# Router logits of an attention and mixture-of-experts kernel: four float32 matmuls against twelve bfloat16 ones on three exact parts

## The chip, the cores and the metric

One core of a Trainium2 chip runs the whole program in one launch. The metric is the device time of an execution in microseconds (us). The engines named below are TensorE (PE, with its weight loads PEld), VectorE (DVE), ScalarE (ACT), GpSimd (POOL) and SyncE (SP), which issues most transfers.

## What is computed

Three layers follow each other: banded attention with a few "sink" keys, a mixture of experts with one expert for each token, and a feed-forward layer with a leaky ReLU. The change lies in the router of the second:

```python
def _moe_ref(x, expert_emb, tau, w1, w2):          # x 1536x512, expert_emb 8x512
    xn = x / (np.linalg.norm(x, axis=-1, keepdims=True) + 1e-06)
    en = expert_emb / (np.linalg.norm(expert_emb, axis=-1, keepdims=True) + 1e-06)
    logits = xn @ en.T / tau
    expert_idx = np.argmax(logits, axis=1)
    ...
    gate_w = probs[np.arange(N), expert_idx]
    for e in range(E):
        mask = expert_idx == e
        h = np.maximum(x[mask] @ w1[e], 0.0)
        out[mask] = gate_w[mask, None] * (h @ w2[e])
```

Tokens go to the expert with the largest logit, so the logits need close to float32 precision.

## The kernel before

**Attention** (function `attention`) takes 2 batches x 2 head groups x 6 query blocks x 4 heads, 96 steps of a software pipeline. A step issues one score (L261, two float32 matmuls), on VectorE the masked scores with their minimum (L266), on ScalarE the exponential a step later (L268), five steps later the transposes of the probabilities (L280, copied by L283) and ten steps later the product with the values (L298, L301) of a block. VectorE then divides by the sums (`finish`: L310, L311, L312), which gives the tile `x` of 128 tokens; with the second head group x has its 512 columns. Between these steps the heads of the next group are transposed (L196) and split (L202, L207, L216, L217).

**The router** handles twelve tiles of 128 tokens, in two batches of six that come with the second head group of each batch of attention. `router_turn` (L690) transposes x in four pieces (L697) into one PSUM tile and copies it to SBUF (ScalarE, L700); `router_logits` (L709) multiplies the four pieces with the turned embeddings `embT` (L716, 128x8), takes the maximum in the pass that reads the logits out of PSUM (L718), and makes the index and one-hot row of the expert (L720 to L724). The last tile, number 11, is turned in two halves. PSUM tiles: four of tag "t" (all transposes), three of tag "sc" (scores, logits, ranks), one for xp.

**After the last tile** `router_rank` and `rank_experts` (L727, L751) count tokens for each expert and write the experts' numbers in the order of work, `eid` (L772). SyncE reads these numbers into registers and issues the loads of the experts' weights (`fetch`, L997) with them; the experts' matmuls (L1079) and the feed-forward layer follow, with the weights split into two parts by ScalarE and VectorE (L1001, L1002).

The order of each engine's instructions in the attention part is not written by hand: the program is scheduled at build time, by dependences and estimated times, so an added operation can move others.

Of the kernel before, what the change touches and what calls it, by code (L numbers as in the profile page):

```python
# [7 lines left out]
F32 = mybir.dt.float32  # L8
F32R = mybir.dt.float32r
BF16 = mybir.dt.bfloat16  # L10
# [5 lines left out]
ALU = mybir.AluOpType  # L16
AX = mybir.AxisListType
# [4 lines left out]
P = 128  # L22
# [3 lines left out]
E = 8  # L26
# [112 lines left out]
def attention(c, ctx):  # L139
# [152 lines left out]
    def value(b, g, i):  # L292
# [25 lines left out]
        if g == 0 and half:  # L318
            later(3, lambda: router_turn(c, t, None, (0, 1)))
        if g == 1:  # L320
            later(3, lambda: router_turn(c, t, None, (2, 3) if half else (0, 1, 2, 3)))
            later(5, lambda: router_logits(c, t))
            if t in RANKS:
                t0 = RANKS[RANKS.index(t) - 1] + 1 if RANKS.index(t) else 0
                if t == NTT - 1:
                    later(7, lambda: rank_experts(c))
                later(7, lambda: router_rank(c, t0, t + 1))
# [13 lines left out]
    load_v(0, 0, 3, 3)  # L341
    first, second = group_turns(0, 0)
    setting = router_setup(c, ctx)
    stir(7)
    n = len(items)
# [248 lines left out]
def router_setup(c, ctx):  # L594


    nc, tc = c.nc, c.tc
    cp = c.const
    rp, emb, tau = c.embs
# [10 lines left out]
    t = c.pst.tile([P, 4, E], F32, tag="t", name="embT_ps")  # L610
    for kk in range(4):
        nc.tensor.transpose(t[:, kk, :], emb[:, kk * P:(kk + 1) * P], c.ident[0:E, 0:E])
    c.embT = cp.tile([P, 4, E], F32, name="embT")
    nc.vector.tensor_copy(c.embT, t)

    yield
    c.tri = cp.tile([P, P], BF16, name="tri")
# [69 lines left out]
    return y  # L687


def router_turn(c, t, pool=None, parts=(0, 1, 2, 3)):  # L690

    nc = c.nc
    pool = pool or c.pst
    x = c.x[t].rearrange("p h d -> p (h d)")
    tp = pool.tile([P, len(parts), P], F32, tag="t", name=f"xTp{c.uid()}")
    for k, kk in enumerate(parts):
        turned = nc.tensor.transpose(tp[:, k, :], x[:, kk * P:(kk + 1) * P], c.ident)  # L697
    if parts[0] == 0:
        c.xT[t] = c.rt.tile([P, 4, P], F32, tag="xT" if parts[-1] == 3 else "xTh", name=f"xT{c.uid()}", bufs=2 if parts[-1] == 3 else 1)
    first = nc.scalar.copy(out=c.xT[t][:, parts[0]:parts[-1] + 1], in_=tp)  # L700
    if parts[-1] == 3:
        c.x.pop(t)
        c.xT[t] = c.xT[t], turned
        sq = c.rt.tile([P, DM], F32, tag="sq", name=f"sq{c.uid()}", bufs=1)
        with c.tc.issue_after(first.ins):
            nc.scalar.activation(out=sq, in_=x, func=AF.Square, accum_out=c.ss[:, t:t + 1])


def router_logits(c, t, pool=None):  # L709

    nc = c.nc
    xT, turned = c.xT.pop(t)
    lp = (pool or c.psc).tile([P, E], F32, tag="sc", name=f"lg{c.uid()}")
    with c.tc.issue_after(turned.ins):
        for kk in range(4):
            nc.tensor.matmul(lp, lhsT=xT[:, kk, :], rhs=c.embT[:, kk, :], start=(kk == 0), stop=(kk == 3))  # L716
    lg, top, idx, oh = c.lg[:, t, :], c.top[:, t], c.idx[:, t:t + 1], c.oh[:, t, :]
    nc.vector.tensor_scalar(out=lg, in0=lp, scalar1=0.0, scalar2=None, op0=ALU.add, op1=ALU.max, accum_out=top)  # L718
    hit = c.rt.tile([P, E], F32, tag="hit", name=f"hit{c.uid()}")
    nc.vector.scalar_tensor_tensor(out=hit, in0=lg, scalar=top, in1=c.em8, op0=ALU.is_equal, op1=ALU.mult)  # L720
    nc.vector.tensor_reduce(out=idx, in_=hit, axis=AX.X, op=ALU.min)
    nc.vector.tensor_scalar(out=oh, in0=c.em8, scalar1=idx, scalar2=None, op0=ALU.is_equal)
    if t + 1 < NTT:
        nc.vector.tensor_tensor(out=c.cum[:, t + 1, :], in0=c.cum[:, t, :], in1=oh, op=ALU.add)  # L724
# [807 lines left out]
```

## Time and profile before

| | |
|---|---|
| median of 3 runs | 617.88 us (617.36 to 618.19) |
| the profiled execution | 617.09 us |
| its span, first to last instruction | 615.3 us |
| TensorE busy | 590.1 us (96%) |
| VectorE busy | 390.6 us (63%) |
| ScalarE busy | 288.8 us (47%) |
| mean granted TensorE clock | 0.97 of full speed |

Of the page, the busy shares say which engine is full over the whole span, and the chain of waits which engine's work ended last, step by step back from the end. A share over the span mixes stages; the table of stretches gives the busy time of each engine within one. The timeline gives single instructions with start and duration; neighbours on an engine can overlap a little.

### The profile page before, as it was taken

The numbers are of one execution on the slowest core, as the hardware profiler recorded it, in microseconds if no ns is written. First come the engines' busy times: TensorE is split into PE (matmuls) and PEld (weight loads), VectorE is DVE, ScalarE is ACT, GpSimd is POOL, SyncE is SP. The second block draws the span as 40 slices with busy tenths as digits, with TensorE's granted clock in tenths as the row PEclk, the third lists the DMA queues.
The fourth block names the chain that finished last, engine by engine and source line by source line (L and its number), as shares of the span: only waits on it lengthen the run. The fifth ranks groups of instructions, "written<-read, shape, count | busy, mean of one in ns | idle before, by whom it ended". The sixth has DMA issues, their size and how long they took to land.

```text
span 615.3 us, 9556 instructions
## 1 busy us (share of the span) xinstructions
PE 590.1 (96%) x3411; PEld 512.6 (83%) x3412; DVE 390.6 (63%) x915; ACT 288.8 (47%) x522; POOL 54.2 (9%) x156
## 2 busy tenths in 40 slices
PE   7899999997699999999999999999999999999996
PEld 4799999895499998889989888888888888888884
DVE  7889788856699659997974699964322223322240
ACT  4777787755688444624753445333312222322130
POOL 3011013003122010001000000000100001100001
PEclk7899999996699999999999999999999999999998
DMA  5777570013999593369599600000100000100001
GB/s 121 180 164 169 136 170 2 2 57 115 339 359 312 187 315 116 123 222 364 174 322 347 273 0 2 0 1 0 69 1 1 0 1 17 52 1 1 0 13 60
DMA packets 87991, 73.66 MB, mean 120 GB/s; under 512 B 54024, under 2 KB 70408, under 8 KB 87936
## 3 DMA queue, kind: packets, MB, share of 16 engines
q1 hardware_dynamic: 85824, 66.22, 34.7%
q0 software_dynamic: 2112, 6.75, 3.1%
q8 instruction: 29, 0.48, 0.3%
q14 instruction: 26, 0.21, 0.1%
HBM read 66.67 MB, written 6.29 MB: 119 GB/s over the span
## 4 chain that ended last, share of the span: by engine, by line
PE 88%; DMA 5%; DVE 3%; issue 1%; ACT 1%; POOL 0%; SPq 0%; POOLq 0%; DVEq 0%
PE hp L1079 32%; PE acc L1079 31%; PE xp L298 6%; PE sc L261 4%; DMA slot_raw<-in_moe_w 3%; PE tp L280 3%; PE acc L1188 2%; PE hp L1176 2%; PE lg L716 1%; PE tq L196 1%; PE xp L301 1%; PE xTp L697 1%; PE tr L1068 1%; PE tk L196 1%; DVE p L266 1%
## 5 line engine op out<-in xcount | busy, mean ns | idle before, releaser
L1079 PE MATMUL acc<-slot,h 128*128 128x512 f32 x588 | 146.2, 396 | 1.3 <-issue 1.3
L1079 PE MATMUL hp<-fxT,slot 128*128 128x512 f32 x576 | 140.9, 396 | 0.0
L1079 PEld LDWEIGHTS acc<-slot,h 128*128 128x128 f32 x588 | 109.8, 188 | 27.4 <-issue 1.5
L1079 PEld LDWEIGHTS hp<-fxT,slot 128*128 128x128 f32 x576 | 108.1, 188 | 26.2
L1426 DVE TENSOR_TENSOR lk<-hp,lk 128x512 f32<-128x512 f32 x48 | 32.9, 690 | 103.4 <-ACT lk L1425 103.3
L1425 ACT ACTIVATE lk<-hp 128x512 f32<-128x512 f32 x48 | 28.5, 598 | 119.9 <-PE hp L1079 111.3
L1002 DVE TENSOR_TENSOR slot<-slot_raw,slot 128x1024 fp32r<-128x1024 f32 x48 | 58.4, 1222 | 12.2 <-ACT slot L1001 11.5
L1001 ACT CAST slot<-slot_raw 128x1024 fp32r<-128x1024 f32 x48 | 50.1, 1049 | 19.7 <-DMA slot_raw<-in_moe_w 19.4
L268 ACT ACTIVATE p<-p,los 128x288 f32<-128x288 f32 (+2 forms) x96 | 45.7, 506 | 16.8 <-DVE los L266 16.1
L1079 PE MATMUL acc<-h,slot 128*128 128x256 f32 (+2 forms) x288 | 49.0, 319 | 0.0
L261 PE MATMUL sc<-head_k,head_q 128*128 128x288 f32 (+1 forms) x192 | 43.8, 338 | 4.0 <-DVE head_k L207 2.2
L1079 PEld LDWEIGHTS acc<-h,slot 128*128 128x128 f32 x288 | 43.1, 188 | 2.9
L298 PE MATMUL xp<-v,pt 128*128 128x65 f32 x352 | 43.8, 269 | 0.0
L298 PEld LDWEIGHTS xp<-v,pt 128*128 128x128 f32 x352 | 42.6, 192 | 0.1
L1428 DVE TENSOR_TENSOR h<-lk,h 128x512 fp32r<-128x512 f32 x43 | 29.5, 690 | 18.0 <-ACT h L1427 17.9
L1460 POOL DMA_INDIRECT out_y<-y,sid x12 | 11.7, 978 | 317.5 <-DVE y L1459 295.9
L1427 ACT CAST h<-lk 128x512 fp32r<-128x512 f32 x43 | 26.7, 622 | 27.1 <-DVE lk L1426 27.1
L261 PEld LDWEIGHTS sc<-head_k,head_q 128*128 128x128 f32 x192 | 29.8, 201 | 7.3 <-ACT head_q L216 3.4
L1079 PE MATMUL hp<-slot_big,slot 128*128 128x256 f32 (+1 forms) x192 | 35.4, 334 | 0.0
L1079 PEld LDWEIGHTS hp<-slot_big,slot 128*128 128x128 f32 x192 | 29.8, 189 | 2.7
L280 PE MATMUL tp<-ident,p 128*128 128x128 f32 x176 | 30.2, 278 | 0.0
L1095 POOL DMA_INDIRECT rows<-xd,ids x16 | 18.3, 1142 | 114.4 <-PE tr L1068 109.1
(252 smaller groups left out, 850.5 us busy)
## 6 DMA issues: line engine op xcount, KB each, us to landing
slot_raw<-in_moe_w SPq DMA_DIRECT2D x56, 512.0 KB
slot_wide<-in_moe_w_in SPq DMA_DIRECT2D x8, 1024.0 KB
slot_wide<-in_moe_w_out SPq DMA_DIRECT2D x8, 1024.0 KB
raw_q<-in_q SPq DMA_DIRECT2D x64, 96.0 KB
slot_first<-in_moe_w SPq DMA_DIRECT2D x8, 512.0 KB
raw_k<-in_k SPq DMA_DIRECT2D x32, 96.0 KB
xd<-x SPq DMA_DIRECT2D x12, 256.0 KB
v<-in_v SPq DMA_DIRECT2D x12, 192.0 KB
```

Of the source, the lines that this page charges most:

```text
L261: nc.tensor.matmul(sc[:, 0:w], lhsT=qt[:, half, i * P:(i + 1) * P], rhs=kt[:, off:off + w], start=half == 0, stop=half == 1)
L268: later(1, lambda: nc.scalar.activation(out=p, in_=p, func=AF.Exp, scale=-1.0, bias=lo))
L280: nc.tensor.transpose(u.t[:, h % 2, n, :], u.p[:, h, o:o + P], c.ident)
L298: nc.tensor.matmul(xp[:, h, :], lhsT=u.pt[h // 2][:, h % 2, n, :], rhs=vT[b, g][:, kb, h, :], start=h == 0 and n == 0, stop=h == 3 and i < ...
L1001: nc.scalar.copy(out=sl.g[0], in_=sl.raw)
L1002: nc.vector.tensor_tensor(out=sl.g[1], in0=sl.raw, in1=sl.g[0].bitcast(F32), op=ALU.subtract)
L1079: c.nc.tensor.matmul(out, lhsT=a[x], rhs=b[y], start=first and n == 0, stop=last and n == 2)
L1095: c.nc.gpsimd.indirect_dma_start(out=t[0:w], out_offset=None, in_=c.xd[:, :], in_offset=bass.IndirectOffsetOnAxis(ap=c.ids[0:w, q0 + k:q0 ...
L1425: nc.scalar.activation(out=raw, in_=hp, func=AF.Copy, scale=0.01)
L1426: nc.vector.tensor_tensor(out=raw, in0=hp, in1=raw, op=ALU.max)
L1427: x = nc.scalar.copy(out=h[:, 0, :], in_=raw)
L1428: y = nc.vector.tensor_tensor(out=h[:, 1, :], in0=raw, in1=h[:, 0, :].bitcast(F32), op=ALU.subtract)
```

## The change

The embeddings are split once into three bfloat16 parts that sum to the float32 value. Each tile of x is split the same way while it leaves PSUM: ScalarE casts it to bfloat16, VectorE subtracts that from the original (`left`, float32); the upper 16 bits of each number of `left` are the second part, read in place with a step of two; VectorE subtracts them, which gives the third. Three groups of four bfloat16 matmuls, one for each part of x, multiply with all three parts of the embeddings at once (24 columns). VectorE sums the three results of each expert and takes the maximum in a pass of its own. The first part and the last share a tile of tag "xT" with two buffers, `left` has two of its own; tile 11's separate buffer of tag "xTh" is gone.

```diff
@@ router_setup
     c.embT = cp.tile([P, 4, E], F32, name="embT")
     nc.vector.tensor_copy(c.embT, t)
+    c.emb3 = cp.tile([P, 4, 3, E], BF16, name="emb3")
+    left = rp.tile([P, 4, E], F32, name="emb_left")
+    nc.scalar.copy(out=c.emb3[:, :, 0], in_=t)
+    nc.vector.tensor_tensor(out=left, in0=c.embT, in1=c.emb3[:, :, 0], op=ALU.subtract)
+    nc.scalar.copy(out=c.emb3[:, :, 1], in_=left)
+    nc.vector.tensor_tensor(out=c.emb3[:, :, 2], in0=left, in1=c.emb3[:, :, 1], op=ALU.subtract)
@@
+def upper(t):
+
+    return t.bitcast(BF16).rearrange("p k (n t) -> p k n t", t=2)[:, :, :, 1]
@@ router_turn
     if parts[0] == 0:
-        c.xT[t] = c.rt.tile([P, 4, P], F32, tag="xT" if parts[-1] == 3 else "xTh", name=f"xT{c.uid()}", bufs=2 if parts[-1] == 3 else 1)
-    first = nc.scalar.copy(out=c.xT[t][:, parts[0]:parts[-1] + 1], in_=tp)
+        c.xT[t] = (c.rt.tile([P, 2, 4, P], BF16, tag="xT", name=f"xT{c.uid()}", bufs=2),
+                   c.rt.tile([P, 4, P], F32, tag="xl", name=f"xl{c.uid()}", bufs=2))
+    two, left = c.xT[t]
+    some = slice(parts[0], parts[-1] + 1)
+    mid = upper(left)[:, some]
+    first = nc.scalar.copy(out=two[:, 0, some], in_=tp)
+    nc.vector.tensor_tensor(out=left[:, some], in0=tp, in1=two[:, 0, some], op=ALU.subtract)
+    nc.vector.tensor_tensor(out=two[:, 1, some], in0=left[:, some], in1=mid, op=ALU.subtract)
@@ router_logits
-    lp = (pool or c.psc).tile([P, E], F32, tag="sc", name=f"lg{c.uid()}")
+    lp = (pool or c.psc).tile([P, 3, E], F32, tag="sc", name=f"lg{c.uid()}")
+    parts = [two[:, 0], upper(left), two[:, 1]]
     with c.tc.issue_after(turned.ins):
-        for kk in range(4):
-            nc.tensor.matmul(lp, lhsT=xT[:, kk, :], rhs=c.embT[:, kk, :], start=(kk == 0), stop=(kk == 3))
+        for n, x in enumerate(parts):
+            for kk in range(4):
+                nc.tensor.matmul(lp.rearrange("p a e -> p (a e)"), lhsT=x[:, kk, :], rhs=c.emb3[:, kk].rearrange("p a e -> p (a e)"),
+                                 start=n + kk == 0, stop=n + kk == 5)
-    nc.vector.tensor_scalar(out=lg, in0=lp, scalar1=0.0, scalar2=None, op0=ALU.add, op1=ALU.max, accum_out=top)
+    nc.vector.tensor_reduce(out=lg, in_=lp.rearrange("p a e -> p e a"), axis=AX.X, op=ALU.add)
+    nc.vector.tensor_reduce(out=top, in_=lg, axis=AX.X, op=ALU.max)
```

In the rows of the new order below, L717 and L718 are the two subtractions of `router_turn` (`xl` is `left`), L739 and L740 the sum and the maximum of `router_logits`, and all lines of the program after L612 stand some lines lower than before (the one-hot steps L720 to L724 are L742 to L746, the rank steps L736 to L743 are L758 to L765).

VectorE where the first batch's last two tiles meet the scores of attention, before: L721 to L724 finish the tile before, L266 are masked scores, L207 and L217 head splits.

```order
L721 TENSOR_REDUCE idx<-hit_1533 128x1
L207 TENSOR_TENSOR head_k_142<-tk_1552,head_k_142 64x384
L266 ISA p_1503,los<-sc_1558,mb 128x288
L266 ISA los 128x1
L207 TENSOR_TENSOR head_k_144<-tk_1552,head_k_144 64x384
L722 TENSOR_SCALAR oh<-em_685,idx 128x8
L724 TENSOR_TENSOR cum<-cum,oh 128x8
L266 ISA p_1582,los<-sc_1583,mc 128x288
L266 ISA los 128x1
L266 ISA p_1582,los<-sc_1626,mc 128x288
```

The same place now:

```order
L717 TENSOR_TENSOR xl_1553<-xTp_1547,xT_1552 128x512
L312 TENSOR_TENSOR x_1001<-xp_1578,rec_1583 128x256
L266 ISA p_1560,los<-sc_1609,mb 128x288
...
L744 TENSOR_SCALAR oh<-em_691,idx 128x8
L217 SCALAR_TENSOR_TENSOR head_q_143<-tq_1690,head_q_143 128x384
L718 TENSOR_TENSOR xT_1552<-xl_1553 128x512
L746 TENSOR_TENSOR cum<-cum,oh 128x8
L717 TENSOR_TENSOR xl_1638<-xTp_1632,xT_1637 128x512
L310 TENSOR_SCALAR rec_1712<-xp_1702 128x4
L718 TENSOR_TENSOR xT_1637<-xl_1638 128x512
L266 ISA p_1651,los<-sc_1652,mc 128x288
```

Four subtractions over 128x512, two tiles' worth, now stand between the last scores of one query block (mask `mb`) and the first of the next (`mc`).

VectorE at the last two tiles now; x_2081 is tile 11, xl_2475 tile 10, xl_2108 the second half of tile 11:

```order
L717 TENSOR_TENSOR xl_2475<-xTp_2469,xT_2474 128x512
L310 TENSOR_SCALAR rec_2486<-xp_2481 128x4
L758 TENSOR_TENSOR sel_2458<-rk_2455,oh 128x32
L718 TENSOR_TENSOR xT_2474<-xl_2475 128x512
L311 RECIPROCAL rec_2486<-rec_2486 128x4
L759 TENSOR_REDUCE r<-sel_2458 128x4
L312 TENSOR_TENSOR x_2081<-xp_2481,rec_2486 128x256
L762 TENSOR_TENSOR ge_2461<-t_695,r 128x44
L739 TENSOR_REDUCE lg<-lg_2487 128x8
...
L717 TENSOR_TENSOR xl_2108<-xTp_2511,xT_2107 128x256
L744 TENSOR_SCALAR oh<-em_691,idx 128x8
L718 TENSOR_TENSOR xT_2107<-xl_2108 128x256
```

Before, the L310 to L312 of tile 11 had only the rank steps between them; now both subtractions of tile 10 stand ahead of tile 11's L312.

## Rows read from the trace of the kernel before

**Rows 1.** The page, parts 1 and 4: busy time by engine; the chain by engine.
```profile
PE 590.1 (96%) x3411; PEld 512.6 (83%) x3412; DVE 390.6 (63%) x915; ACT 288.8 (47%) x522; POOL 54.2 (9%) x156
PE 88%; DMA 5%; DVE 3%; issue 1%; ACT 1%; POOL 0%; SPq 0%; POOLq 0%; DVEq 0%
```

**Rows 2.** Stretches: from:to length, busy PE, PEld, DVE, ACT, POOL, clock, DMA, GB/s.
```profile
60.00:97.00 37.00, 37.00 (x324) 36.37 (x323) 31.02 (x132) 30.03 (x72) 4.13 (x21) 1.00 0.52 130
61.70:84.10 22.40, 22.40 (x197) 21.97 (x195) 16.97 (x72) 17.55 (x44) 1.99 (x11) 1.00 0.54 144
84.10:96.00 11.90, 11.90 (x110) 11.90 (x108) 11.38 (x51) 10.93 (x27) 1.76 (x8) 1.00 0.53 122
97.00:120.00 23.00, 22.44 (x179) 20.90 (x178) 20.38 (x83) 16.74 (x40) 5.90 (x11) 1.00 0.01 2
120.00:137.00 17.00, 17.00 (x149) 16.68 (x148) 8.87 (x45) 10.12 (x28) 0.59 (x2) 1.00 0.13 47
137.00:146.00 9.00, 8.26 (x69) 7.87 (x68) 5.69 (x34) 3.41 (x9) 1.78 (x3) 0.91 0.23 88
```

**Rows 3.** Timeline (start, duration), and the last row from the chain.
```profile
148.46 0.15 DVE L772 CAST eid<-ef 1x8 int32<-1x8 f32 x1
149.63 25.95 SPq L997 DMA_DIRECT2D slot_raw<-in_moe_w  x19
...
153.98 9.55 DMA slot_raw<-in_moe_w
```

**Rows 4.** Timeline, TensorE: one tile's logits and the instruction after.
```profile
87.13 0.96 PE L716 MATMUL lg<-embT,xT 128*128 128x8 f32 x8
87.94 0.42 PE L697 MATMUL xTp<-ident,x 128*128 128x128 f32 x2
```

**Rows 5.** 16-bit weight loads: timeline of L791, and line L896 (min/median/max ns).
```profile
150.90 0.42 PEld L791 LDWEIGHTS <-slot_u 128*128 128x128 f16 x11 [0.27 <-issue]
151.24 0.13 PEld L1273 LDWEIGHTS <-hot 128*128 128x128 bf16 x2
...
L896 PEld LDWEIGHTS <-hot x12: 95/98/98, 284.0 to 284.4; 128*128 128x128 bf16 x12
```

**Rows 6.** Groups of instructions, VectorE, 0 to 170 us: busy us, mean ns, idle before.
```profile
L718 DVE TENSOR_SCALAR_CACHE_REDUCE lg<-lg 128x8 f32<-128x8 f32 x12 | 2.0, 165 | 1.6 <-PE cnt L759 0.8 <-PE lg L716 0.6
L721 DVE TENSOR_REDUCE idx<-hit 128x1 f32<-128x8 f32 x12 | 1.9, 159 | 0.1
L1073 DVE TENSOR_TENSOR mxT<-tr,mxT 128x512 fp32r<-128x512 f32 x1 | 0.7, 692 | 2.2 <-ACT mxT L1072 2.2
L1231 DVE TENSOR_TENSOR h<-th,h 128x256 fp32r<-128x256 f32 x1 | 0.4, 419 | 0.0
L834 DVE TENSOR_REDUCE mn<-ee 128x8 f32<-128x64 f32 x1 | 0.2, 220 | 0.0
```

**Rows 7.** Timeline, VectorE: a copy over 128x512 and what follows it.
```profile
87.56 0.69 DVE L283 COPY pt<-tp 128x512 f32<-128x512 f32 x1
88.15 0.16 DVE L718 TENSOR_SCALAR_CACHE_REDUCE lg<-lg 128x8 f32<-128x8 f32 x1
```

**Rows 8.** Timeline, the last tiles: tile 9's cast, tile 10's x, tile 11.
```profile
138.25 0.59 ACT L700 COPY xT<-xTp 128x512 f32<-128x512 f32 x1 [2.16 <-PE xTp L697]
...
140.88 0.42 DVE L312 TENSOR_TENSOR x<-xp,rec 128x256 f32<-128x256 f32 x1
...
143.09 0.42 DVE L312 TENSOR_TENSOR x<-xp,rec 128x256 f32<-128x256 f32 x1
...
143.57 0.44 PE L697 MATMUL xTp<-ident,x 128*128 128x128 f32 x2
...
144.04 0.37 ACT L700 COPY xT<-xTp 128x256 f32<-128x256 f32 x1 [1.00 <-PE xTp L697]
...
145.53 0.17 DVE L718 TENSOR_SCALAR_CACHE_REDUCE lg<-lg 128x8 f32<-128x8 f32 x1 [0.82 <-PE cnt L759]
```

**Rows 9.** Timeline, VectorE: the first batch's first rank step.
```profile
97.52 0.21 DVE L736 TENSOR_TENSOR sel<-rk,oh 128x48 f32<-128x48 f32 x1
```

More of the change, by code (lines that the diff above doesn't have):

```diff
@@ L698, in router_turn @@
     if parts[0] == 0:
-        c.xT[t] = c.rt.tile([P, 4, P], F32, tag="xT" if parts[-1] == 3 else "xTh", name=f"xT{c.uid()}", bufs=2 if parts[-1] == 3 else 1)
-    first = nc.scalar.copy(out=c.xT[t][:, parts[0]:parts[-1] + 1], in_=tp)
+        c.xT[t] = (c.rt.tile([P, 2, 4, P], BF16, tag="xT", name=f"xT{c.uid()}", bufs=2),
[6 more added lines that the diff above has]
+    nc.vector.tensor_tensor(out=two[:, 1, some], in0=left[:, some], in1=mid, op=ALU.subtract)
     if parts[-1] == 3:
         c.x.pop(t)
-        c.xT[t] = c.xT[t], turned
+        c.xT[t] = two, left, turned
         sq = c.rt.tile([P, DM], F32, tag="sq", name=f"sq{c.uid()}", bufs=1)
@@ L711, in router_logits @@
     nc = c.nc
-    xT, turned = c.xT.pop(t)
-    lp = (pool or c.psc).tile([P, E], F32, tag="sc", name=f"lg{c.uid()}")
+    two, left, turned = c.xT.pop(t)
+    lp = (pool or c.psc).tile([P, 3, E], F32, tag="sc", name=f"lg{c.uid()}")
+    parts = [two[:, 0], upper(left), two[:, 1]]
     with c.tc.issue_after(turned.ins):
-        for kk in range(4):
-            nc.tensor.matmul(lp, lhsT=xT[:, kk, :], rhs=c.embT[:, kk, :], start=(kk == 0), stop=(kk == 3))
+        for n, x in enumerate(parts):
+            for kk in range(4):
+                nc.tensor.matmul(lp.rearrange("p a e -> p (a e)"), lhsT=x[:, kk, :], rhs=c.emb3[:, kk].rearrange("p a e -> p (a e)"),
+                                 start=n + kk == 0, stop=n + kk == 5)
     lg, top, idx, oh = c.lg[:, t, :], c.top[:, t], c.idx[:, t:t + 1], c.oh[:, t, :]
-    nc.vector.tensor_scalar(out=lg, in0=lp, scalar1=0.0, scalar2=None, op0=ALU.add, op1=ALU.max, accum_out=top)
+    nc.vector.tensor_reduce(out=lg, in_=lp.rearrange("p a e -> p e a"), axis=AX.X, op=ALU.add)
+    nc.vector.tensor_reduce(out=top, in_=lg, axis=AX.X, op=ALU.max)
     hit = c.rt.tile([P, E], F32, tag="hit", name=f"hit{c.uid()}")
```

## The prediction

> **What bounds the kernel now.** I read the page first: engine shares and the chain of waits [rows 1]. TensorE is busy 96% of the span and holds 88% of the chain, so work taken off it can count, but only where it is the last to arrive. Then the stretches [rows 2]. The router's twelve tiles come in two batches of six: the first within 60 to 97 us, the second from 123 to 146 us. In both the reader is to compare TensorE with VectorE. From 60 to 97 us TensorE is busy 37.0 of 37.0 us, but VectorE 31.0 as well, and within it from 84.1 to 96 us VectorE is busy 11.38 of 11.90: both engines are full there. From 120 to 137 us TensorE is full and VectorE has 8.1 us free. From 137 us on neither is full; there one tile's chain of steps sets the pace.
>
> What follows the router hangs on it: SyncE reads the expert numbers that VectorE writes at 148.46 us, and only then issues the loads of the experts' weights (from 149.63 us), one of which is the 9.55 us DMA link of the chain [rows 3]. Whatever moves the expert numbers moves all that comes after, so I count the shift of that one instruction and carry it to the end.
>
> **What a tile saves on TensorE.** Four float32 matmuls are eight records, from 87.13 us to the next instruction at 87.94: 0.81 us [rows 4]. Twelve 16-bit ones with their weight loads: the twelve float16 matmuls at L791 take turns 34 ns apart (eleven loads with starts and ends in 0.42 us from 150.90, the next work loads at 151.24), and twelve bfloat16 loads at full clock start within 0.4 us, 284.0 to 284.4 [rows 5]. I take 0.42 us, so the saving is 0.39 us a tile. No row has weights read with a step, as those of the second part are here (every other bfloat16); between 34 ns and the 99 ns of a float32 record (0.79/8 by rows 4) four such loads add 0 to 0.26 us a tile. I take 0, since the number of weights in a load stays the same, and keep the other end (+0.8 over three tiles where TensorE is last).
>
> A rule of the Trainium skill speaks against the change here: "TensorE: Matmul & The Clock Gate", LDWEIGHTS (loading the stationary operand), has a load's time go by its columns, P/1.2 ns, whatever the width that streams past. By that formula alone, estimated, 128 columns are 107 ns, twelve loads 1.28 us, and each tile would lose 0.47 us instead of gaining 0.39. The trace disagrees with it for 16-bit weights: 34 ns a pair [rows 5]; the same page's section on fast weight load names a quicker path for full 128-column weights that are not float32, packed or with a step.
>
> **What a tile adds on VectorE.** Two subtractions over 128x512 and a second small reduction. The nearest subtraction, from PSUM against an SBUF tile, takes 692 ns for 512 columns and 419 for 256 [rows 6]. In a packed stretch an instruction starts before the one ahead has ended: a 0.69 us copy is followed 0.59 us later [rows 7]. The first subtraction I count 0.59, the second, which needs the first's result, 0.66: 1.25 us. For the reductions, 165 ns (one pass with the maximum accumulated) become a sum over 24 numbers, between the 159 ns of 8 and the 220 ns of 64, and a maximum of 159 that waits for it [rows 6]: +0.2. So 1.45 us a tile, 8.7 us a batch, against a saving of 2.3 us a batch on TensorE. ScalarE's copy keeps its shape and count, only its output is narrower: nothing.
>
> **Setup.** Four small operations on 128x32 split the embeddings in the crowded stretch before 60 us. Two on VectorE at 160 to 220 ns [rows 6]: +0.3; ends 0 and 0.7 (if ScalarE's two stand in the way as well).
>
> **First batch.** By the new order, the subtractions of four tiles and the reductions of three fall in 61.7 to 84.1 us: 4 x 1.25 + 3 x 0.2 = 5.6 us. VectorE is idle there for 22.40 - 16.97 = 5.4 us [rows 2]. In the full stretch 4% still stayed idle (0.52 of 11.90); with 4% of 22.4, 1.0 us, left unusable, 4.4 us can be filled, and 1.2 are left over. The other two tiles' subtractions and three reductions fall in 84.1 to 96 us, which has no room: 2 x 1.25 + 3 x 0.2 = 3.1 us. Together +4.3 us. TensorE's 2.3 us give nothing back, as VectorE is then last. Ends: if VectorE may run behind and catch up until 120 us, it must fit 31.0 + 20.4 + 8.7 = 60.1 us into 60: +0.1. If none of the idle time can be used, +8.7. I stay near the middle: an attention score has three PSUM tiles, so TensorE cannot run far ahead of a late VectorE, and x waits in one of four PSUM tiles until its first subtraction is done.
>
> **Second batch, 120 to 137 us.** Three tiles' 4.4 us on VectorE lie in its 8.1 free us; TensorE, which is last, saves 3 x 0.39: -1.2 us (ends -1.2 and 0).
>
> **The last tiles.** In the new order tile 10's two subtractions stand ahead of the last two steps of tile 11's attention output (x, at 143.09 us now [rows 8]), and tile 9's ahead of tile 10's. I walk it with the durations above. Tile 9's cast ends at 138.84 [rows 8]; a copy and tile 8's small steps stand ahead of its first subtraction (139.05 to 139.7), and with one more between the second ends near 140.6. Two steps later tile 10's x starts at 141.4 instead of 140.88 [rows 8], and tile 10's cast ends at 142.9. Its first subtraction runs 143.0 to 143.7, the second from 144.0 to 144.7 with two small steps of others between, and tile 11's x starts at 144.85, 1.76 later. From x to the reduction of the last logits are 2.44 us now (143.09 to 145.53): x, transpose, cast, matmuls. Then: the same to the cast's end, 0.41 each for two half subtractions with a step of tile 10 ahead, and four matmuls instead of four float32 ones: 2.9, +0.46. The separate maximum: +0.2. Sum +2.4 us. Ends: +0.4 (only the last tile's own steps count) and +4.4 (1.45 for each of tiles 9, 10 and 11). Tile 11, turned in two halves, now holds one of the two buffers from early on, so tiles 6 to 10 share the other; in the walk each cast comes over 1 us after the matmuls that free it, so I add nothing.
>
> After 148 us the order differs only in a few weight splittings that swap places while the weights still load; the 9.55 us DMA link covers them [rows 3]. Without it a swap costs one 1.2 us splitting at most.
>
> **Sum.** 0.3 + 4.3 - 1.2 + 2.4 = +5.8 us. The profiled execution took 617.09 (span 615.3), 0.79 below the median of 617.88; 617.09 becomes 622.9, and the median 623.7. All low ends together give -0.7 us, all high ends +13.8. About 0.2%, 1.2 us, is what a measurement of this kernel can tell from no change.
>
> **The rivals.**
> - *VectorE catches up, and TensorE's saving counts.* For it: VectorE has 6.0 us idle in 60 to 97 us and 2.6 in 97 to 120 [rows 2], and the chain there names TensorE. Against it: 8.7 us do not fit into 6.0, and the steps that would lag feed the scores. It decides if the added 8.7 us delay TensorE's next input nowhere before 137 us; then nine tiles save 0.39 each, -3.5 us, the end costs +0.9 (the last tile's own steps and a part of tile 10's), and -2.6 gives 615.3. Faster: 0.10.
> - *Half of that.* VectorE's lag is won back by 120 us (+0.1), TensorE saves 1.2, the end costs +1 to +2: between -0.1 and +0.9, 618.3. Within 0.2%: 0.12.
> - *TensorE stalls on the new waits.* The three groups of four matmuls wait for the cast and each subtraction in turn, and all other matmuls and transposes queue behind them. Where VectorE is late, each of twelve tiles then holds TensorE, not only the full stretch. With +8.7 in the first batch and +4.4 at the end, no saving between: +13.4, 631.3. For it: both engines are full at 84 to 96 us. Against it: the order puts scores or transposes between the groups in most tiles. 0.08.
> - *Weight loads by their columns*, as the rule above has it, would take TensorE 0.47 us a tile more where it is last: +1.4 instead of -1.2 in 120 to 137 us, and the sum +8.4, 626.3. By rows 5 it is improbable: 0.02, and inside the range.
> - *The change does nothing*: excluded, as the new order has 12 x 12 of the new matmuls and none of the old outside the rare path.
>
> **Numbers.** The forecast has 0.68, and with the two slower rivals 0.78 for slower. Its range goes from 618.9 (+1.0: first batch nearly hidden, the end at +1.2) to 629.7 (+11.8: two thirds of the high ends); that leaves out the faster rival, most of the unchanged one and the worst stall, some 0.2. Faster 0.10, same 0.12, slower 0.78.
>
> **What would show it.** Right: VectorE over 95% busy from 62 to 97 us and the first rank step (L736 of before, at 97.52 us [rows 9]) near 102; TensorE with idle slices there, ended by VectorE; a tile's logits at 0.42 us of TensorE; subtractions at 0.6 to 0.7 us; the expert numbers near 154.3 instead of 148.46 us; the rest of the span as long as now. Wrong: expert numbers at or before 148.5 us, TensorE still at 100% from 60 to 97 us, or a shift that arises after the weights' loads.

## The result and the profile after

| | before | changed |
|---|---|---|
| median of 5 runs | 617.88 us (617.36 to 620.03) | 621.14 us (619.32 to 621.47) |
| the profiled execution | 617.09 us, span 615.3 | 619.32 us, span 617.5 |

The ratio is 1.0051 (95% interval 1.0029 to 1.0074), so the change costs 3.2 us (1.8 to 4.6): slower, inside the range of 618.9 to 629.7, with a little over half of the 5.8 us that the sum gave.

The page of the changed kernel, parts 1 and 4, answers to [rows 1]:

```profile
PE 589.1 (95%) x3460; PEld 507.2 (82%) x3460; DVE 403.7 (65%) x943; ACT 289.0 (47%) x524; POOL 56.0 (9%) x156
PE 83%; DVE 6%; DMA 4%; ACT 4%; issue 1%; POOL 0%; POOLq 0%; SPq 0%; ACTq 0%; DVEq 0%
```

VectorE has 13.1 us more work. Of the chain, TensorE's share fell from 88 to 83%; VectorE's rose from 3 to 6% and ScalarE's from 1 to 4%. The change touches ScalarE only by a narrower output and two small casts, so its new share is a first sign of a cost that the forecast did not have.

The stretches, with the columns of [rows 2]:

```profile
60.00:97.00 37.00, 36.08 (x341) 33.10 (x340) 34.82 (x129) 29.78 (x73) 4.17 (x22) 1.00 0.53 135
61.70:84.10 22.40, 22.22 (x216) 20.92 (x215) 20.89 (x80) 17.36 (x45) 1.74 (x10) 1.00 0.56 146
84.10:96.00 11.90, 11.15 (x104) 9.64 (x104) 11.68 (x41) 10.23 (x25) 1.75 (x9) 1.00 0.49 125
97.00:120.00 23.00, 22.67 (x181) 21.36 (x181) 20.91 (x95) 16.68 (x40) 5.85 (x10) 1.00 0.01 1
120.00:137.00 17.00, 17.00 (x170) 16.38 (x169) 13.98 (x53) 10.18 (x28) 0.59 (x2) 1.00 0.12 47
137.00:146.00 9.00, 5.99 (x69) 5.04 (x68) 7.81 (x37) 3.41 (x9) 2.12 (x3) 0.82 0.24 90
```

As forecast, VectorE is nearly full up to 97 us (94%, a little under the 95% that was named, and 98% from 84.1 to 96), TensorE, full before, has 0.9 us idle there, and from 120 to 137 us VectorE takes 5.1 us more work beside a full TensorE.

The timeline of TensorE for one tile's logits, against [rows 4] (L736 is the new matmul; xT is packed, xl is read with a step):

```profile
139.01 0.25 PE L736 MATMUL lg<-emb,xT 128*128 128x24 bf16 x4
139.09 0.17 PEld L736 LDWEIGHTS <-xl 128*128 128x128 bf16 x4
139.11 0.25 PE L736 MATMUL lg<-emb,xl 128*128 128x24 bf16 x4
139.19 0.17 PEld L736 LDWEIGHTS <-xT 128*128 128x128 bf16 x4
139.21 0.25 PE L736 MATMUL lg<-emb,xT 128*128 128x24 bf16 x4
```

A group of four follows the last by 0.10 us. So by the measure that gave 0.81 us in [rows 4], from the first start to the start of the next instruction, the twelve take about 0.3 us; their last end, which the profile models, comes 0.45 us after the first start. Four loads with a step take the 0.17 us of four packed ones.

The groups on VectorE, 0 to 170 us, with the columns of [rows 6] (the forms of whole and half tiles are mixed in L717 and L718):

```profile
L718 DVE TENSOR_TENSOR xT<-xl 128x512 bf16<-128x512 f32 (+1 forms) x13 | 8.5, 656 | 0.1
L717 DVE TENSOR_TENSOR xl<-xTp,xT 128x512 f32<-128x512 f32 (+1 forms) x13 | 8.4, 649 | 3.6 <-ACT xT L716 3.4
L739 DVE TENSOR_REDUCE lg<-lg 128x8 f32<-128x24 f32 x12 | 2.1, 176 | 0.3 <-PE cnt L781 0.3
L740 DVE TENSOR_REDUCE top<-lg 128x1 f32<-128x8 f32 x12 | 1.9, 157 | 0.1
```

The timeline of the last tiles, against [rows 8], with the expert numbers of [rows 3] at its end:

```profile
139.62 0.42 DVE L312 TENSOR_TENSOR x<-xp,rec 128x256 f32<-128x256 f32 x1
...
141.24 0.69 DVE L717 TENSOR_TENSOR xl<-xTp,xT 128x512 f32<-128x512 f32 x1 [0.20 <-ACT xT L716]
...
142.01 0.68 DVE L718 TENSOR_TENSOR xT<-xl 128x512 bf16<-128x512 f32 x1
...
142.81 0.42 DVE L312 TENSOR_TENSOR x<-xp,rec 128x256 f32<-128x256 f32 x1
...
145.78 0.18 DVE L739 TENSOR_REDUCE lg<-lg 128x8 f32<-128x24 f32 x1 [0.25 <-PE cnt L781]
...
149.07 0.15 DVE L794 CAST eid<-ef 1x8 int32<-1x8 f32 x1
```

Tile 10's two subtractions stand ahead of tile 11's x, as the forecast had it: from x to x it is now 3.19 us, 2.21 before.

**A table of markers.** The same instruction can be found in each trace. One at 56.98 us of before, ahead of the router, comes 0.96 us earlier in the trace of the changed kernel. That is chance: four kernels below (changed, e1, e5, e9) have the same instructions up to the load stage, and it lay at -0.96, +1.23, -0.22 and -0.08 in them. So each row of the table is taken against its own marker at 56.98; the columns up to 143 us agree in those four within 0.1 us. Entries are us later (+) than in the trace of before: the first rank step [rows 9], x at 122.35, tile 10's and tile 11's x [rows 8], the expert numbers [rows 3], the first h of the experts on VectorE, and the first expert's result (yT). Each row is one execution; those of e3, e9 and e10 were the slowest of their kernels, 1.6, 3.6 and 2.1 us above the median.

| kernel | 97.5 | 122.4 | 140.9 | 143.1 | eid 148.5 | h 167.2 | yT 205.0 |
|---|---|---|---|---|---|---|---|
| changed | +4.1 | +0.7 | -0.3 | +0.7 | +1.6 | +3.5 | +3.1 |
| e1 sixth cast back | +4.1 | +0.7 | -0.4 | +0.6 | +1.1 | +3.5 | +2.7 |
| e2 before, casts ahead | 0.0 | 0.0 | 0.0 | 0.0 | 0.0 | +2.4 | +3.3 |
| e3 subtractions alone | +2.2 | +2.3 | +2.2 | +3.2 | +3.5 | +3.3 | +4.4 |
| e4 matmuls alone | -0.9 | -2.4 | -3.4 | -3.4 | -3.5 | -3.3 | -3.1 |
| e5 changed, casts as before | +4.1 | +0.7 | -0.3 | +0.7 | +1.6 | +3.1 | +4.5 |
| e6 tiles 0 to 5 new | +4.1 | +0.7 | +0.7 | +0.7 | +1.0 | +1.0 | +1.0 |
| e7 tiles 6 to 11 new | 0.0 | 0.0 | -1.1 | -0.1 | +0.4 | +0.5 | +1.3 |
| e8 tiles 6 to 9 new | 0.0 | 0.0 | -1.1 | -1.1 | -1.5 | -1.4 | -1.7 |
| e9 changed, casts late | +4.2 | +0.7 | -0.3 | +0.7 | +1.6 | +1.8 | +8.3 |
| e10 e8, casts late | 0.0 | 0.0 | -1.1 | -1.1 | -0.6 | -1.5 | -0.2 |
| e11 before, casts late | 0.0 | 0.0 | 0.0 | 0.0 | 0.0 | -1.0 | -1.8 |
| e12 GpSimd's part | +2.2 | +0.5 | -0.5 | -0.5 | -0.5 | -1.3 | +0.6 |

The first row tells where the 3.2 us come from: 0.7 are lost by 122 us, 1.0 is gained by 141 us, the last tiles lose 1.9, and from the expert numbers to the first h another 1.9 is lost, in a stage where the change has no instruction.

Two columns want care. The rank step at 97.5 us ends the router's own chain for the batch, not attention's: at the same time the scores of attention (97.9 us of before) are 3.0 us late in the changed kernel and its next x (98.2 us) 1.2. From 119 us on scores and x agree (+0.7), so the first batch is read at 122.4 us.

The expert numbers move with the granted TensorE clock too. From tile 11's x to `eid` the changed kernel takes 6.26 us, all at 0.50 (1.2 GHz), but e1, with the same instructions up to there, 5.82 us at a mean of 0.67 (2.4 GHz in a part of it). With float32 logits in the last tiles, before takes 5.37 us at 0.62, e10 5.83 at 0.51, and e8, the same instructions as e10, 4.97 at 0.85. So up to 0.9 us in the column `eid` is a matter of the execution. At like clocks (changed against e10; e7, 5.82 at 0.63, against before) the three parts cost 0.4 to 0.45 us in this piece; the other 0.4 to 0.5 of the 0.9 us that the changed kernel lost there go with the clock. What sets the clock in one execution was not shown; up to 143 us TensorE had 0.97 to 1.00, and from there to 146 us it was busy 1.60 of 3.00 us in the changed kernel, 2.40 in before.

**That loss.** ScalarE's timeline, and TensorE's th, of the kernel before:

```profile
163.56 1.05 ACT L1001 CAST slot<-slot_raw 128x1024 fp32r<-128x1024 f32 x1 [1.34 <-DMA slot_raw<-in_moe_w]
164.51 0.38 ACT L1222 ACTIVATE hr<-hp 128x256 f32<-128x256 f32 x1
164.92 1.05 ACT L1001 CAST slot<-slot_raw 128x1024 fp32r<-128x1024 f32 x1
164.94 0.69 PE L1228 MATMUL th<-ident,hr 128*128 128x128 f32 x2 [1.33 <-ACT hr L1222]
```

and of the changed one:

```profile
163.92 1.04 ACT L1023 CAST slot<-slot_raw 128x1024 fp32r<-128x1024 f32 x1 [1.63 <-DMA slot_raw<-in_moe_w]
165.29 1.04 ACT L1023 CAST slot<-slot_raw 128x1024 fp32r<-128x1024 f32 x1 [0.33 <-DMA slot_raw<-in_moe_w]
166.24 0.38 ACT L1244 ACTIVATE hr<-hp 128x256 f32<-128x256 f32 x1
166.68 0.69 PE L1250 MATMUL th<-ident,hr 128*128 128x128 f32 x2 [3.00 <-ACT hr L1244]
```

The program's scheduler, which orders each engine by dependences and estimated times, put the sixth cast of a weight slot ahead of `hr`, the first expert's relu. Both casts wait for their loads (1.63 and 0.33 us), the relu waits behind them, and TensorE's wait for it grew from 1.33 to 3.00 us. Behind the fifth cast alone `hr` could have started at about 164.87 us; the sixth cost it 1.37 us, 0.95 of its own time and the rest mostly the wait. The next cast then stood ahead of the first `h` in the same way and waited 0.84 us for its load.

### The profile page after: what moved, and what is told of

Its sections match the earlier page's. It is cut to its first block, busy times and chain, and to the rows that moved or that the text cites. A ratio compares the mean times of both kernels' runs of the same rounds, so it can differ in the third digit from the quotient of the medians.

```text
span 617.5 us, 9679 instructions
## 1 busy us (share of the span) xinstructions
PE 589.1 (95%) x3460; PEld 507.2 (82%) x3460; DVE 403.7 (65%) x943; ACT 289.0 (47%) x524; POOL 56.0 (9%) x156
## 4 chain that ended last, share of the span: by engine, by line
PE 83%; DVE 6%; DMA 4%; ACT 4%; issue 1%; POOL 0%; POOLq 0%; SPq 0%; ACTq 0%; DVEq 0%
PE hp L1101 31%; PE acc L1101 30%; PE xp L298 5%; PE hp L1198 3%; PE acc L1210 3%; DMA slot_raw<-in_moe_w 3%; PE sc L261 3%; PE tp L280 2%; DVE p L266 1%; ACT p L268 1%; PE tq L196 1%; ACT yT L1517 1%; PE xp L301 1%; PE tr L1090 1%; DVE head_k L207 1%
## 5 line engine op out<-in xcount | busy, mean ns | idle before, releaser
L298 PE MATMUL xp<-v,pt 128*128 128x65 f32 x352 | 42.4, 272 | 0.0
L1117 POOL DMA_INDIRECT rows<-xd,ids x16 | 20.1, 1259 | 114.3 <-PE tr L1090 111.0
```

The source lines that it names most:

```text
L298: nc.tensor.matmul(xp[:, h, :], lhsT=u.pt[h // 2][:, h % 2, n, :], rhs=vT[b, g][:, kb, h, :], start=h == 0 and n == 0, stop=h == 3 and i < ...
L1117: c.nc.gpsimd.indirect_dma_start(out=t[0:w], out_offset=None, in_=c.xd[:, :], in_offset=bass.IndirectOffsetOnAxis(ap=c.ids[0:w, q0 + k:q0 ...
```

## The experiments

All times are medians, and each ratio is against runs of the kernel before on the same chip (medians 618.0, 618.0 and 618.1 us in the three groups; single runs lie between 616.5 and 620.4). The profiled execution of before, 617.09 us, is 0.9 below them, so a time and the last column of the table can differ by about 1 us.

**e1, e2: the place of one cast.** e1 defers the sixth cast of the changed kernel:

```diff
-    c.work.pop(Q0)
+    c.work.pop(5)
+    c.sixth = c.work.queues[0].pop(0)[1]
+    c.work.pop(Q0)
...
-        nc.scalar.activation(out=hr, in_=hp, func=AF.Relu)
+        x = nc.scalar.activation(out=hr, in_=hp, func=AF.Relu)
+        if flow.now == 0:
+            with c.tc.issue_after(x.ins):
+                c.sixth()
```

> The changed kernel with one pair on ScalarE put back: the sixth cast of the first expert's weight slots is issued behind the first hr (the relu between the first two matmul groups of the narrow expert), as in the kernel before; nothing else of the first 160 us is touched. Theory A (the swap of hr and a cast that waits for its DMA costs about 1.1 to 1.4 us): the wait of TensorE ahead of the first th falls from 3.0 us to about 1.4 us, eid to th falls from 17.6 to about 16.4 us, and the time is about 619.8 us, 1.3 below the changed kernel, 0.3% above the kernel before. Theory B (the landing of the slots' loads sets the end of this stage whatever the order): the wait moves to the next matmul groups, the time stays at 621.1 us, within 0.4.

Measured: 621.66 us (ratio 1.0054, 1.0036 to 1.0073), no gain; TensorE still waited 2.93 us ahead of th. In this execution the load of the fifth cast, which stands ahead of `hr` in the kernel before too, landed at 166.16 us, 15.4 us after the expert numbers; and the seventh cast had moved ahead of the first h. The edit undid half of the difference in order, and Theory A was not told from B. The mirror is cleaner:

```diff
-        nc.scalar.copy(out=sl.g[0], in_=sl.raw)
+        c.casts = getattr(c, "casts", []) + [nc.scalar.copy(out=sl.g[0], in_=sl.raw)]
...
-        nc.scalar.activation(out=hr, in_=hp, func=AF.Relu)
+        with c.tc.issue_after(c.casts[5].ins) if flow.now == 0 else nullcontext():
+            nc.scalar.activation(out=hr, in_=hp, func=AF.Relu)
```

> The mirror: the kernel before, its float32 logits untouched, with the sixth cast forced ahead of the first hr on ScalarE; by this all later casts move up one place as in the changed kernel. Theory A: +1.1 to +1.4 us, 619.1 us, with TensorE's wait ahead of th at about 3 us instead of 1.33. Theory B: 617.9 us, within 0.4.

Measured: 620.02 us, ratio 1.0029 (1.0017 to 1.0041): +1.8 us (1.1 to 2.5). Up to the expert numbers the two traces agree within 0.05 us; then:

```profile
163.91 1.04 ACT L1001 CAST slot<-slot_raw 128x1024 fp32r<-128x1024 f32 x1 [1.50 <-DMA slot_raw<-in_moe_w]
165.28 1.04 ACT L1001 CAST slot<-slot_raw 128x1024 fp32r<-128x1024 f32 x1 [0.32 <-DMA slot_raw<-in_moe_w]
166.23 0.38 ACT L1223 ACTIVATE hr<-hp 128x256 f32<-128x256 f32 x1
166.66 0.69 PE L1229 MATMUL th<-ident,hr 128*128 128x128 f32 x2 [2.85 <-ACT hr L1223]
```

The same picture as in the changed kernel, without any change of the router. Theory A holds for the kernel before, with a size at its upper end or above.

The table tells the same of this stage over all traces, by its column h less its column `eid`. With the casts as in before it is -0.2 to +0.2 us in e3, e4, e6, e7 and e8, though their expert numbers come from 3.5 us early to 3.5 us late. With casts moved up it is +1.9 (changed) and +2.4 (e1, e2), and with the casts late about -0.9 (e10, e11, e12). Two traces do not fit, e5 (about +1.5, with the casts as in before) and e9 (+0.2, with late casts); in both a load came late. In e5 the fifth load landed 15.9 us after the expert numbers, in the nine others whose fifth cast waited for it after 14.8 to 15.4 us; e9's fourth cast could start only after 15.2 us, in every other trace it started by 13.1. The issue of the loads follows the expert numbers alike (1.17 us in before, changed and e5), so a late `eid` by itself does not lengthen this stage.

**e3, e4: the two halves of the change.** e3 adds the two subtractions to the kernel before, read by nobody; e4 takes them out of the changed kernel and multiplies the first part three times instead, so its logits lack the other parts, and behind the expert numbers tokens may go to other experts than in the rest:

```diff
 e3
+    nc.vector.tensor_tensor(out=c.dead_left[:, some], in0=tp, in1=upper(c.xT[t])[:, some], op=ALU.subtract)
+    nc.vector.tensor_tensor(out=c.dead_low[:, some], in0=c.dead_left[:, some], in1=upper(c.dead_left)[:, some], op=ALU.subtract)
 e4
-    nc.vector.tensor_tensor(out=left[:, some], in0=tp, in1=two[:, 0, some], op=ALU.subtract)
-    nc.vector.tensor_tensor(out=two[:, 1, some], in0=left[:, some], in1=mid, op=ALU.subtract)
...
-    parts = [two[:, 0], upper(left), two[:, 1]]
+    parts = [two[:, 0]] * 3
```

> The kernel before with its float32 logits, and the two subtractions of each tile added on VectorE with results that nobody reads: about 1.3 us more of VectorE work a tile, no wait of the logits on them. Theory A (the lag of VectorE in the first batch is made up between 97 and 120 us, and what stays comes from the last tiles and the swap of casts): the score operations at 97 us are 2 to 3 us late, those at 120 us under 1 us, the end 0.3 to 1.0 us late, 618.5 us. Theory B (VectorE's extra work at its full stretch stays in the time): +3 us or more still at 120 us and at the end, 621 us.

> The changed kernel without its two subtractions: all three groups of four matmuls read the cast of x, so the second and third part of x are left out. TensorE has its shorter logits, VectorE only 0.2 us more a tile. Theory A (the 0.39 us a tile is worth something only where TensorE is the bound, in the second batch from 120 to 137 us and in the last tiles): about 1.2 us less there, 616.6 us, the score operations at 97 us unmoved within 0.4. Theory B (TensorE's saving is hidden everywhere, since another engine or a DMA ends the waits): 617.9 us, within 0.4. Theory C (the saving counts for all twelve tiles): 4.7 us less, 613.2 us.

Measured: e3 621.56 us, ratio 1.0056 (1.0034 to 1.0077), +3.5 us: the time of Theory B, with a lag of 2.3 instead of 3 us at 122.4. That lag was 2.2 at 97.5 us, so VectorE makes up nothing by itself. e4 615.48 us, ratio 0.9958 (0.9940 to 0.9976), -2.6 us, between Theories A and C: the marked instructions had gained 0.9 at 97.5 us, 2.4 at 122.4 and 3.4 at 140.9. Six tiles at 0.39 are 2.3 and three more 1.2: each of the first nine tiles gives its saving back, the last two or three nothing (-3.4 to -3.5 from there to the expert numbers). The stretches of e3, then of e4, 60 to 97 and 97 to 120 us:

```profile
60.00:97.00 37.00, 36.17 (x309) 35.04 (x308) 34.52 (x138) 29.15 (x70) 3.47 (x18) 1.00 0.52 130
97.00:120.00 23.00, 22.44 (x183) 21.18 (x183) 20.48 (x79) 16.73 (x40) 6.26 (x13) 1.00 0.01 2
```

```profile
60.00:97.00 37.00, 36.97 (x370) 35.86 (x368) 32.46 (x138) 30.93 (x75) 4.44 (x23) 1.00 0.52 131
97.00:120.00 23.00, 22.51 (x181) 21.02 (x180) 19.02 (x83) 17.68 (x42) 5.59 (x10) 1.00 0.01 1
```

In e3 VectorE is as full as in the changed kernel (34.52 and 34.82 us) and TensorE has 0.8 us idle up to 97 us, as there 0.9, but nothing is shorter for it afterwards. Added, the two give -0.1 at 122.4 and 0.0 at the expert numbers, where the changed kernel has +0.7 and +1.6. What neither has is logits that wait for the splitting; 0.8 us in the first batch and 0.8 more in the last tiles, by difference, would be theirs. No run shows this by itself, and 0.4 to 0.5 of the second 0.8 go with the clock.

**e5: the order of casts restored.** Each of the sixth to fourteenth casts gets a fixed place (e9 to e12 use the same helper, from the fifth cast on and one place later):

```diff
+def cut_after(c, x, *left):
+    if len(c.cuts) in left:
+        with c.tc.issue_after(x.ins):
+            c.cuts.pop(0)()
...
-    c.work.pop(Q0)
+    c.work.pop(5)
+    c.cuts = [x[1] for x in c.work.queues[0]]
+    c.work.queues[0].clear()
...
-        nc.scalar.activation(out=hr, in_=hp, func=AF.Relu)
+        cut_after(c, nc.scalar.activation(out=hr, in_=hp, func=AF.Relu), 9, 7, 5, 3)
...
```

> The changed kernel with the first 14 casts of weight slots on ScalarE in the places that they had in the kernel before (the first run put back one of them, and the next cast moved up ahead of the h of the first th instead). Theory A (the order of the casts, worth 1.8 us in the mirror, is the same 1.8 us here): 619.4 us, TensorE's wait ahead of the first th about 1.4 us. Theory B (the whole difference is made before 149 us, by the router, and the order adds nothing to it): 621.1 us, within 0.5.

Measured: 621.49 us, ratio 1.0047 (1.0030 to 1.0063): Theory B's time, but not its reason. The expert numbers come 1.6 us late here too, the fifth cast's load landed at 165.68 us, 0.8 later after them than in before, and `hr` behind it still cost TensorE 2.62 us. Later the scheduler had set the next expert's casts ahead of `y`, the copy of the first expert's sum, and TensorE waited 1.3 us for that.

**e6, e7, e8: which tiles.** A set `NEW` of tiles takes the three parts, the others the float32 matmuls; e7 and e8 hold the casts as in e5, in e6 they stand so by themselves.

```diff
+NEW = range(0, 6)     # e6; e7: range(6, 12); e8: range(6, 10)
...
+    if t in NEW:
+        first = nc.scalar.copy(out=two[:, 0, some], in_=tp)
...
+    else:
+        first = nc.scalar.copy(out=left[:, some], in_=tp)
...
```

> The changed kernel with the three parts for tiles 0 to 5 (the first batch) alone; tiles 6 to 11 have the float32 logits of the kernel before, and the casts stand as in the kernel before. Theory A (the new way costs VectorE's lag up to 97 us and gets most of it back in the stretch to 120 us, where TensorE is the bound and its logits are shorter): about 3 us late at 97 us, 0.7 us at 122 us, 618.7 us at the end. Theory B (the forecast's: what is lost by 97 us stays lost): 3 us late at 122 us too, 621 us.

> The three parts for tiles 6 to 11 (the second batch) alone, the first batch with float32 logits, the casts held in the order of the kernel before. Theory A (TensorE's saving gives about 1 us between 122 and 141 us, the splitting on the path of the last two tiles takes about 1.9 us): 1 us early at 141 us, 0.9 us late at eid, 618.8 us. Theory B (the last tiles' waits cost nothing that the loads behind eid do not hide): 617.0 us.

> The three parts for tiles 6 to 9 alone, where TensorE is the bound and VectorE has room; the first batch and the last two tiles have float32 logits, the casts are held in the order of the kernel before. Theory A: 0.8 to 1.2 us early at 141 us and at eid, and so 616.9 us. Theory B (the start of the slots' loads or their landing does not move with eid): 617.9 us, within 0.4.

Measured: e6 619.92 us, ratio 1.0032 (1.0018 to 1.0045); e7 620.11 us, 1.0031 (1.0019 to 1.0043); e8 616.64 us, 0.9985 (0.9972 to 0.9998). In the traces Theory A holds in all three up to the expert numbers: e6 is 4.1 us late at 97.5 us and 0.7 at 122.4; e7 gains 1.05 by 140.9 and is 0.4 late at the expert numbers (0.9 was expected); e8 keeps its gain and is 1.5 early there (0.6 in e10, with the same instructions at a lower clock). The columns of e6 and e7 add up to those of the changed kernel within 0.15 us as far as that. The times of e6 and e7 are 1.2 to 1.3 us above what was expected; part of that comes after the experts' first h, where e7's `y` stood behind casts again (TensorE waited 0.8 us; the 0.4 in e6 left no lag at 205 us). More arises in the feed-forward layer, between the results at 428 and at 597 us: 1.5 us in e6's trace and 0.7 in e7's, 0.2 in that of the changed kernel. Why stays open.

**e9 to e12: the casts late.**

> The changed kernel with each cast of a weight slot from the fifth to the fourteenth one place later on ScalarE than in the kernel before, so that the first hr stands behind four casts instead of six and the first h behind five. Theory A (what the load stage lost, 1.9 us between eid and the first h, is lost by a relu that stands behind a cast whose DMA has not landed): TensorE's wait ahead of the first th falls from 3.0 to about 1.0 us, the first h comes 1.5 to 2 us earlier against eid, and the time is 619.4 us. Theory B (the slots' loads, whose DMA engines are full in this stage, set its end, and the wait moves on to the matmuls that need the slots): 621.2 us, within 0.5.

> The three parts for tiles 6 to 9 alone, which gave 616.64 us with the casts as in the kernel before, now with the casts one place later. Theory A: the fifth cast waited until 163.21 us and hr stood behind it to 164.16; that goes, 0.5 to 0.9 us less, 616.0 us. Theory B: 616.6 us, within 0.4.

> The kernel before, float32 logits untouched, with the casts one place later. Theory A: hr starts at about 163.7 instead of 164.51 us, 0.5 to 0.8 us less, 617.4 us. Theory B: 618.0 us, within 0.4.

Measured: e11 616.07 us, ratio 0.9970 (0.9958 to 0.9982): -1.9 us (1.1 to 2.6) from the order of casts alone, more than Theory A's 0.8. Its timeline:

```profile
163.73 0.38 ACT L1230 ACTIVATE hr<-hp 128x256 f32<-128x256 f32 x1 [1.42 <-PE hp L1086]
164.01 1.04 ACT L1001 CAST slot<-slot_raw 128x1024 fp32r<-128x1024 f32 x1
164.17 0.69 PE L1236 MATMUL th<-ident,hr 128*128 128x128 f32 x2 [0.47 <-ACT hr L1230]
```

`hr` now waits for its own matmuls alone. e10: 616.17 us, 0.9967 (0.9954 to 0.9979), where A expected 616.0 and B 616.6, both within the interval; and it is no better than e11: beside late casts the three parts in tiles 6 to 9 show no gain of their own. e9: 621.91 us, 1.0067 (1.0048 to 1.0086), no gain. TensorE's waits in e9 from 158 to 206 us (total, times, longest), and ScalarE's timeline:

```profile
PE ty L1285 <- ACT y L1278: 4.8, 1, 4.8
...
PE th L1258 <- ACT hr L1252: 0.5, 1, 0.5
```

```profile
181.14 1.05 ACT L1023 CAST slot<-slot_raw 128x1024 fp32r<-128x1024 f32 x1 [1.49 <-DMA slot_raw<-in_moe_w]
185.22 1.04 ACT L1023 CAST slot<-slot_raw 128x1024 fp32r<-128x1024 f32 x1 [3.03 <-DMA slot_raw<-in_moe_w]
186.17 0.58 ACT L1278 COPY y<-acc 128x512 f32<-128x512 f32 x1
```

The wait for `hr` fell to 0.5 us and the first h came 1.7 us earlier, as Theory A says. Then two casts of the next expert's slots, which e9 does not pin, stood ahead of `y` and took 4.8 us in this execution (the slowest of six, 625.48 us). So the wait moved on, but not because TensorE's matmuls lacked their slots, as B had it: it is the same trap a few instructions later, and here waiting is most of the price (1.49 and 3.03 us). In e11 `y` stands ahead of those casts.

> The three parts for tiles 0 to 9, float32 logits for the last two, casts one place later, and in tiles 0 to 5 the second subtraction (the third part, read and written in SBUF alone) on GpSimd, which is busy 4 of the 37 us from 60 to 97 us: 0.7 us less of VectorE a tile. GpSimd's price for 128x512 with two operands stands in no row; its copy of 128x128 took 0.295 us, four times that is 1.2 us. Theory A (VectorE's work is what makes the first batch late, and GpSimd's is beside it): under 1.5 us late at 97 us, 0.5 to 1.5 us early at 122 us, 1 us below the run with tiles 6 to 9 alone. Theory B (GpSimd's subtraction is late or slows VectorE's own, and the first batch stays about 0.7 us late at 122 us): 0.7 us above it.

```diff
-        nc.vector.tensor_tensor(out=two[:, 1, some], in0=left[:, some], in1=mid, op=ALU.subtract)
+        (nc.gpsimd if t < 6 else nc.vector).tensor_tensor(out=two[:, 1, some], in0=left[:, some], in1=mid, op=ALU.subtract)
```

Measured: 620.37 us, ratio 1.0042 (1.0027 to 1.0057), 4.2 above e10. GpSimd's group of subtractions, with the columns of [rows 6]:

```profile
L722 POOL TENSOR_TENSOR xT<-xl 128x512 bf16<-128x512 f32 x6 | 6.2, 1042 | 9.2 <-DVE top L747 3.9 <-DVE xl L721 3.7 <-DVE rec L310 1.6
```

It halves the lag of the rank step at 97.5 us (2.2 for 4.1) but leaves 0.5 of 0.7 us at 122.4. The expert numbers come 0.5 us early; that is lost by 205 us, again with `y` behind casts (TensorE waited 1.3 us), and 1.9 us more in the feed-forward layer between 428 and 597 us, as in e6. Neither theory's time came out, because of what follows the router.

## Why the prediction was right, and where its sizes were off

Slower was right, and the likeliest case was the one that happened. Each term of the sum, forecast and measured against the start marker (the second row of the first batch is the one that counts in the sum; the third takes in the forecast's +0.5 for tile 10's x, so that it ends where the markers do; the last row goes to the last result of the feed-forward layer, 605.28 us in before):

| term | forecast | measured |
|---|---|---|
| setup | +0.3 | not resolved |
| first batch, up to 97.5 us | +4.3 | +4.1 |
| the same, up to 122 us | +4.3 | +0.7 |
| second batch and tile 10's x, 122 to 141 us | -0.7 | -1.0 |
| last tiles, 141 us to the expert numbers | +1.9 | +1.9 |
| weight loads, to the first h | 0 | +1.9 |
| after that | 0 | -0.2 |
| sum | +5.8 | +3.3 |

- **Unit prices.** The saving on TensorE was taken as 0.39 us a tile. By starts alone it is about 0.5 (0.3 against 0.81 us): the forecast's 0.42 us ran from a first start to a last end, its 0.81 from start to start. What came back is 0.40 for each of e4's six tiles, so the figure held. The step of two costs nothing, so the low end was the right choice. The subtractions take 0.69 us each on a whole tile, the sum 176 ns and the maximum 157. VectorE's busy time grew by 13.1 us over twelve tiles, 1.09 a tile, where 1.45 was forecast.
- **Setup.** The marker behind it lies at +0.1 on the mean of the ten kernels with the new setup, single ones between -1.1 and +1.2; a cost of 0.3 is neither seen nor excluded.
- **First batch: the step that failed** is "TensorE's 2.3 us give nothing back, as VectorE is then last". The rank step came 4.1 us late for 4.3, as the text's sign had it, but attention was not that late (1.2 to 3.0 us), so this agreement is in part luck; by 122 us 0.7 is left, and e6 shows the same +0.7 for this batch alone. The saving of all six tiles counted: e4 gains 2.4 us by 122.4. e3, with the same subtractions and float32 logits, keeps its whole lag of 2.3, itself less than the 3.1 that the forecast's sum gives without the reductions. The forecast priced the batch by the engine that was last in it, as if the saving of the other vanished; by 122 us most of it had counted. That it counts where TensorE is last again, behind 97 us, is an argument; no run separates it. The rival of half the lag won back had this place right, but gave VectorE as the reason.
- **Second batch.** -1.0 for -0.7: e7 and e8, with this batch alone, show the same 1.05. The half microsecond by which tile 9's subtractions were to delay tile 10's x did not appear.
- **Last tiles.** The mechanism was the one described: tile 10's subtractions stand ahead of tile 11's x. From x to x the walk gave 3.45 us and 3.19 were measured; from x to the last sum 2.9 and 2.97. That the term came out at +1.9 is luck in part: 1.0 is the later x (e7 has it, e8 does not), 0.4 to 0.45 the tile's own steps, and the rest goes with the clock, which the walk left as it was. e8, which spares the last two tiles, is 1.8 us earlier at the expert numbers than e7, and e10, with the same instructions at a lower clock, 1.0.
- **After 148 us: the second step that failed** is "the 9.55 us DMA link covers them ... Without it a swap costs one 1.2 us splitting at most". The link covered nothing, and it was more than one swap: the sixth cast ahead of `hr` cost 1.4 us (1.0 of its own time, 0.4 of waiting), the cast after it 0.8 more ahead of `h` (the fifth load itself had landed 0.25 us earlier than in before), and both fall on TensorE. e2 shows this order alone: 1.8 us by its ratio, 2.4 at the first h. The text's own sign of a wrong forecast, a shift that arises behind the weights' loads, was there, and the expert numbers came 1.6 us late, not 5.8. That the order is what the changed kernel lost 1.9 us by rests on e2, on the five traces with before's order that lose nothing here, and on TensorE's equal wait (3.00 and 2.85 us). Undoing it in the changed kernel itself (e1, e5, e9) brought no time back: e1 undid half, and in e5 and e9 a load came late and other casts stood ahead of `y`. Why the scheduler chose the other order was not tried.

The errors cancelled in part, which is luck: 3.6 us too much in the first batch, 1.9 too little in the load stage. The reason given for the upper end of the range does not come out either: two thirds of 13.8 us are 9.2, not 11.8; nothing measured lies near it. The weight-load rule of the Trainium skill ("TensorE: Matmul & The Clock Gate", LDWEIGHTS section), by which a load goes by its columns, is not borne out for 16-bit weights: four loads took 0.17 us, where its formula would estimate 0.43. The Trainium skill's section on fast weight load, on the same page, agrees with that, packed and with a step.

## What to carry to other kernels

An engine that is held up by another need not lose its own savings: here a batch that VectorE's extra work alone made 2.3 us late (e3) ended only 0.7 us late once TensorE also had less to do, so price a swap of work between two full engines over the whole stretch in which either is the bound. When an edit changes the schedule elsewhere, look at every in-order queue in which a short, urgent instruction (a relu, a copy out of PSUM) can fall behind work that waits for a DMA: the price is what is left of the wait for that DMA and the work itself (0.4 and 1.0 us at one place here, nearly all waiting at another), and pinning such an order gained 1.9 us here (e11, 616.1 us), where the change itself cost 3.2. A marker in one trace can move with the granted clock of that execution; look at the clock before reading a few tenths of a microsecond. The best versions found are the kernel before with the late casts and e10, 0.3% below before; the three parts for all tiles beat it in no run.

## What was not expected of the hardware

- The same first 57 us of instructions ended 1.0 us early to 1.2 us late in the traces of four kernels that share them, and from there these ran in step, within 0.1 us, for 85 us more. A single profile tells changes of 0.1 us only against a marker of its own.
- GpSimd's subtraction of 128x512 numbers in SBUF took 1.04 us, 1.5 times VectorE's 0.69, and VectorE's first subtraction beside it stayed at 687 ns (688 without).
